# First batch's states: two loads at the head of the scalar and sync queues in place of two loads on GpSimd's queue (block-recurrent cross attention, then a softplus-erf feed-forward block)

## The chip, the cores and the metric

The kernel runs on one core of one Trainium2 chip. The metric is the device time of one execution in microseconds (us); less is better. Engines are named as in the profile: PE is TensorE's matmul and PEld its weight load, DVE is VectorE, ACT is ScalarE, POOL is GpSimd, SP is SyncE. A q behind a name (SPq, ACTq) marks an instruction of that engine's sequencer, such as the issue of a DMA. All data are f32.

## The reference, cut to what matters

```python
B, H, S, Ns, D = (8, 8, 512, 32, 64)          # x: (B,H,S,D)   state: (B,H,Ns,D)
scores = scale * np.matmul(x, state.transpose(0, 1, 3, 2))
a = softmax(scores)                            # exp(s - max) / (sum + 1e-9)
xread = np.matmul(a, state)
scores2 = scale * np.matmul(state, x.transpose(0, 1, 3, 2))
a2 = softmax(scores2)
sread = np.matmul(a2, x)
y = np.concatenate([xread, sread], axis=2)     # 544 rows a batch
x = y.transpose(0, 2, 1, 3).reshape(B * 544, H * D)
h = x @ w_in                                   # 4352 x 512 @ 512 x 2048
g = h * erf(softplus(h))
return g @ w_out                               # 2048 x 512
```

Tokens and states read each other (per batch and head), and the 4352 resulting rows go through a feed-forward block with the activation h · erf(softplus(h)).

## The kernel before, in words

**The work as a whole.** One core takes the batches b = 0 to 7 in order, and at the end the 256 state rows of all batches together. The product of attention weights, states and `w_in` is regrouped: `mixed_part` and `mixed_pair` (lines 447 to 474) first multiply the states with `w_in` into tiles `m`, and the hidden rows are then the attention weights `aT` times `m`. Batch 0 uses plain products (`first0` line 761, `project` line 597), later batches a seven-product scheme (`hidden7`, `project7`). While batch 0 is computed, the weights arrive in 1024-KB blocks as raw words (`weight`, line 127) and are converted by two ACT and three DVE instructions each (lines 144 to 150); the block after next is fetched when one is converted (`on_dve`, line 749).

**What sets the order.** Nothing is left to a planner in this part. From line 89 to line 976 the instructions of PE, DVE, ACT and SP stay in the order in which the code names them (`in_order`, line 78, called in line 976). Each engine takes its own list from the front and stops at an instruction whose inputs are not there. POOL has only a few instructions: it makes the 128×128 identity `ident` (`make_identity`, line 64) and, in this version, issues two DMAs.

**The first loads (lines 106 to 113 and 782 to 784).** The states of batch 0 are 64 KB: for e = 0, 1 (heads of even and odd number) a DMA of 32 KB brings 128 rows of 64 elements into one half of the columns of `st[:, 0, :]`. Both are issued by `nc.gpsimd`, line 109. The tokens of batch 0 are four chunks of 128 tokens, c = 0 to 3, of 256 KB each: ACT issues c = 0, then c = 2; SP issues c = 1, then c = 3 (line 112). Behind them SP issues three weight blocks (line 138 through `fetch`). In this text x0 to x3 are these four loads.

**The first attention (`attention0`, lines 292 to 385), by halves t = 0, 1 of the tokens.** This is PE's list from its first instruction on:

| step | line | what | needs |
|---|---|---|---|
| `warm(8)` | 785, 169 | 16 matmuls of `ident` with itself, results unused | `ident` |
| `turn(0)` | 349, 315 | 8 transposes: chunk 1, then chunk 0 | x1, x0 |
| `states` | 350, 182 | 1 transpose of the states; ACT copies it back into `st` (line 183) | both state loads |
| `warm(1)` | 351 | 2 matmuls of `ident` | |
| `score(0)` | 352, 328 | 16 matmuls, first scores | copied states; `xT` half 0 (ACT line 320, DVE line 321) |
| `turn(1)` | 353, 315 | 8 transposes: chunk 2, then chunk 3 | x2, x3 |
| `warm(3)` | 357 | 6 matmuls of `ident` | |
| `score(1)` | 358, 328 | 16 matmuls, second scores | `xT` half 1 (ACT 320, DVE 321) |
| `warm(28)` | 788 | 56 matmuls of `ident`, results unused | |
| `mixed_part` | 802, 471 | 16 matmuls, states by the first `w_in` block | the converted block |

DVE's list beside it: copy of half 0 (321); two transposes of score(0) (334); copy of half 1 (321); maximum and subtraction of half 0 (342, 343); two transposes of score(1) (334); maximum and subtraction of half 1; sums (347) between the conversion steps of the first weight block (147 to 149); normalisation (232 to 235); two transposes into `aT` (371). ACT copies (320, 183, 338), takes exponentials (344) and does its part of the conversions (144, 146).

**Completion of DMAs.** In the built program the DMAs of the ACT and SP queues take eight completion semaphores in turn, in the order of the code; the two of POOL's queue have semaphores of their own. A DMA that takes a semaphore for the second time may have to wait for the first use to end.

Of the kernel before, what the change touches and what calls it, by code (L numbers as in the profile page):

```python
# [16 lines left out]
def kernel(  # L17
# [17 lines left out]
    nc = tc.nc  # L35
    B, H, S, D = x.shape
# [69 lines left out]
    st = const.tile([P, B, P], F32, name="st")  # L106
    x_t[0] = xin.tile([P, NC, H, D], F32, name="x")
    for e in range(2):
        nc.gpsimd.dma_start(out=st[:, 0, D * e:D * e + D],
                            in_=state[0].rearrange("(i e) n d -> e i n d", e=2)[e])  # L110
    for c in range(NC):
        (nc.scalar, nc.sync)[c % 2].dma_start(
            out=x_t[0][:, c], in_=x[0, :, P * c:P * c + P].rearrange("h p d -> p h d"))
# [951 lines left out]
```

## Time and profile before

| what | us |
|---|---|
| median of 3 runs (lowest, highest) | 734.94 (734.78, 735.68) |
| the profiled execution's own time | 734.94 |
| its span in the profile | 733.2 |
| outside the span (difference) | 1.74 |
| PE busy | 721.7 (98%) |
| PEld busy | 588.0 (80%) |
| DVE busy | 524.7 (72%) |
| ACT busy | 396.1 (54%) |
| POOL busy | 2.1 |

Busy time counts the matmuls of `ident`, too, so a busy PE is not always a PE with useful work. The profile's sections are: busy time by engine; the span in 40 equal slices (18.3 us each), a digit for the busy tenths; the DMA queues (q1 is SP's, q10 is ACT's, q0 is POOL's); the chain that ended last; the costliest groups; the DMA issues with the time from issue to landing. "PEclk" is the share of its full clock that TensorE was granted. The trace behind the page also answers for a stretch of time: the instructions in order, each with the idle time of its engine before it and what ended that idle time; the waits, longest first; the DMAs of one line with the least, median and greatest time to landing; the busy times and the granted clock between two points in time. All points in time here count from the start of the span.

### The profile page before, as it was taken

To read this page: it belongs to the slowest core of one execution; us is meant where nothing else is said; L and a number is where in the kernel's file an instruction comes from. 1 tells how busy PE (TensorE), PEld (TensorE's weight loads), DVE (VectorE), ACT (ScalarE), POOL (GpSimd) and SP (SyncE) were. 2 spreads that over 40 slices of the span, in tenths; PEclk is the share of its full clock that TensorE was granted. 3 is DMA by queue.
4 is the path that set the end of the run, shared out by engine and by line. 5 is a ranking of instruction groups with operands and counts; after the bars stand their busy time and mean duration, and the time that the engine had idled before them with its cause. 6 is when DMAs were issued, how large, how long until landed. Compare 5 with 4: busy or idle time off the path is not lost.

```text
span 733.2 us, 12162 instructions
## 1 busy us (share of the span) xinstructions
PE 721.7 (98%) x5032; PEld 588.0 (80%) x5032; DVE 524.7 (72%) x768; ACT 396.1 (54%) x500; POOL 2.1 (0%) x8
## 2 busy tenths in 40 slices
PE   7999999999999999999999999999999999999997
PEld 6534435888889888988989888988898899999996
DVE  3988887997788666867687669866686756675423
ACT  3899884655646445754355445554565434443340
POOL 1000000000000000000000000000000000000000
PEclk9999999999999999999999999999999999999999
DMA  7577752330043202410061104220121000000001
GB/s 234 169 209 239 216 112 58 87 58 31 14 94 74 51 1 47 98 30 30 1 144 23 37 1 87 64 46 10 30 58 30 30 1 30 1 30 1 30 1 29
DMA packets 138998, 46.40 MB, mean 63 GB/s; under 512 B 126512, under 2 KB 130352, under 8 KB 138944
## 3 DMA queue, kind: packets, MB, share of 16 engines
q1 hardware_dynamic: 136576, 44.85, 24.5%
q10 hardware_dynamic: 2272, 0.72, 0.5%
q8 instruction: 39, 0.64, 0.4%
q14 instruction: 15, 0.12, 0.1%
q0 software_dynamic: 96, 0.07, 0.0%
HBM read 33.03 MB, written 8.91 MB: 57 GB/s over the span
## 4 chain that ended last, share of the span: by engine, by line
PE 88%; DVE 4%; ACT 1%; SPq 1%; issue 1%; DMA 0%; DVEq 0%; ACTq 0%
PE o L650 47%; PE h L543 27%; PE o L600 7%; PE at L457 2%; SPq L432 1%; PE h L457 1%; PE h L764 1%; PE at L197 1%; PE at L471 1%; PE h L277 1%; DVE s L777 0%; PE at L277 0%; DVE hs L771 0%; ACT L774 0%; DVE w_out L148 0%
## 5 line engine op out<-in xcount | busy, mean ns | idle before, releaser
L650 PE MATMUL o<-w_out,s 128*128 128x256 f32 x480 | 118.0, 380 | 0.0
L650 PE MATMUL o<-raw,hs 128*128 128x256 f32 x480 | 117.3, 382 | 0.0
L550 ACT ACTIVATE s<-hs 128x512 f32<-128x512 f32 x120 | 75.4, 630 | 74.3 <-DVE hs L551 74.0
L650 PE MATMUL o<-w_out,hs 128*128 128x256 f32 x480 | 114.1, 380 | 0.0
L650 PEld LDWEIGHTS o<-raw,hs 128*128 128x128 f32 x480 | 89.9, 190 | 22.6 <-issue 10.9
L551 DVE TENSOR_TENSOR hs<-hs,h 128x512 f32<-128x512 f32 x90 | 61.8, 688 | 62.5 <-PE h L543 62.4
L650 PEld LDWEIGHTS o<-w_out,hs 128*128 128x128 f32 x480 | 90.8, 190 | 16.3 <-issue 4.2
L650 PEld LDWEIGHTS o<-w_out,s 128*128 128x128 f32 x480 | 84.6, 191 | 7.9
L551 DVE TENSOR_TENSOR hs<-s,h 128x512 f32<-128x512 f32 x60 | 41.1, 685 | 67.6 <-PE h L543 67.2
L543 PEld LDWEIGHTS h<-aT,m 128*128 128x128 f32 x672 | 83.8, 192 | 4.3 <-issue 1.4
L543 PE MATMUL h<-aT,m 128*128 128x128 f32 x672 | 84.4, 275 | 0.0
L595 DVE TENSOR_TENSOR s<-s,hs 128x2048 f32<-128x2048 f32 (+1 forms) x31 | 68.8, 2219 | 20.4 <-ACT s L593 20.4
L554 ACT COPY s<-h 128x512 f32<-128x512 f32 x29 | 17.0, 586 | 107.6 <-PE h L543 107.6
L600 PE MATMUL o<-w_out,s 128*128 128x512 f32 x128 | 59.1, 600 | 0.6 <-DVE s L777 0.5
L543 PE MATMUL h<-sy,sx 128*128 128x128 f32 x448 | 59.4, 275 | 0.0
L543 PEld LDWEIGHTS h<-sy,sx 128*128 128x128 f32 x448 | 56.7, 192 | 2.0 <-issue 0.5
L593 ACT ACTIVATE s<-s 128x2048 f32<-128x2048 f32 x30 | 57.4, 1912 | 0.3
L559 ACT COPY hs<-h 128x512 f32<-128x512 f32 x29 | 17.0, 586 | 74.8 <-PE h L543 74.8
L650 PE MATMUL o<-raw,s 128*128 128x256 f32 x240 | 56.8, 379 | 0.0
L600 PEld LDWEIGHTS o<-w_out,s 128*128 128x128 f32 x128 | 23.1, 190 | 31.1 <-issue 25.8
L650 PEld LDWEIGHTS o<-raw,s 128*128 128x128 f32 x240 | 43.5, 190 | 4.7
L550 ACT ACT_TABLE_LOAD x31 | 39.8, 1283 | 0.6
(140 smaller groups left out, 917.9 us busy)
## 6 DMA issues: line engine op xcount, KB each, us to landing
raw<-in_moe_w_in_dram SPq DMA_DIRECT2D x8, 1024.0 KB, 5.4
raw<-in_moe_w_out_dram SPq DMA_DIRECT2D x8, 1024.0 KB, 5.0
xq<-in_x_dram SPq DMA_DIRECT2D x112, 64.0 KB, 2.5
x<-in_x_dram SPq DMA_DIRECT2D x56, 128.0 KB, 3.0
out_dram<-ot SPq DMA_DIRECT2D x18, 256.0 KB, 2.1
sc<-xT SPq DMA_DIRECT2D x112, 32.0 KB, 1.9
out_dram<-ot SPq DMA_DIRECT2D x28, 128.0 KB, 1.7
x<-in_x_dram ACTq DMA_DIRECT2D x2, 256.0 KB, 6.0
```

The source lines that it names most:

```text
L197: on_pe = nc.tensor.matmul(out=s2[e][q, :], lhsT=st[r, b, q], rhs=xT[r, i, :], start=True, stop=True)
L277: nc.tensor.matmul(out=sr[q, e, :], lhsT=a2T[:, e, c, q], rhs=xt[:, c, 2 * i + e, :], start=(c == 0), stop=(c == NC - 1))
L457: nc.tensor.matmul(out=ps[k][e][q, :], lhsT=st[r, b, q], rhs=w_in[r, 2 * g:2 * g + 2, i, :], start=True, stop=True)
L543: last = nc.tensor.matmul(out=bank[:, q], lhsT=lhsT, rhs=rhs, start=(first and i == 0 and k == 0), stop=(i == GF - 1 and k == len(ops) - 1 ...
L550: nc.scalar.activation(out=s[:, k], in_=hs[:, k], func=ACTF.Softplus)
L551: add = lambda o, x, y: nc.vector.tensor_tensor(o, x, y, op=ALU.add)
L554: copy(m1, p)
L559: copy(c11, p)
L593: nc.scalar.activation(out=s, in_=s, func=ACTF.Erf)
L595: nc.vector.tensor_tensor(s[:, k], s[:, k], hs[:, k], op=ALU.mult)
L600: nc.tensor.matmul(out=acc[r], lhsT=gT[:, i, P * r:P * r + P], rhs=w_out[:, GF * g + i, :], start=(g == 0 and i == 0), stop=(g == NG - 1 a ...
L650: nc.tensor.matmul(out=acc[bank][:, E2 * c:E2 * c + E2], lhsT=lhs[:, i, :], rhs=rhs[:, g, i, :], start=(first and i == 0 and c == 0), stop ...
```

## The change

In the loop over e, the two state loads are issued by ACT (e = 0) and by SP (e = 1) and no longer by GpSimd. The loop stands ahead of the loads of x, so each of the two is the first DMA of its queue. Nothing else is changed.

```diff
     st = const.tile([P, B, P], F32, name="st")
     x_t[0] = xin.tile([P, NC, H, D], F32, name="x")
     for e in range(2):
-        nc.gpsimd.dma_start(out=st[:, 0, D * e:D * e + D],
-                            in_=state[0].rearrange("(i e) n d -> e i n d", e=2)[e])
+        (nc.scalar, nc.sync)[e].dma_start(out=st[:, 0, D * e:D * e + D],
+                                      in_=state[0].rearrange("(i e) n d -> e i n d", e=2)[e])
     for c in range(NC):
         (nc.scalar, nc.sync)[c % 2].dma_start(
             out=x_t[0][:, c], in_=x[0, :, P * c:P * c + P].rearrange("h p d -> p h d"))
```

In the built program the lists of PE and DVE have the same instructions in the same order. ACT's and SP's lists each have one DMA more, at the front; POOL's list has two DMAs fewer, one of which stood between the two steps that make `ident`. The eight completion semaphores are handed out two places later, so the third weight block of SP (`w_out`, the ninth DMA) now takes the semaphore of ACT's state load and the next one that of SP's; from there on each DMA waits for the same predecessors as before.

## The prediction

> **What bounds the kernel now.** I read the page's 40 slices first, then the waits of the first 20 us, then the first 15 us in order of time, engine by engine. The slices (DVE and POOL beside PE):
>
> ```profile
> PE   7999999999999999999999999999999999999997
> DVE  3988887997788666867687669866686756675423
> POOL 1000000000000000000000000000000000000000
> PEclk9999999999999999999999999999999999999999
> ```
>
> PE is full from the second slice on, in an order written by hand, so this change can gain only by starting the full stretch sooner. The first slice (18.3 us) is the one with a hole. What ends the waits of PE there, by the waits up to 14 us:
>
> ```profile
> PE h L182 <- DMA st<-in_state_dram: 2.7, 1, 2.7
> PE o L169 <- POOL ident masks.py:199: 2.5, 1, 2.5
> ```
>
> Both go back to POOL, and both instructions are touched. PE, ACT and DVE in order of time (start, length, instruction, idle time before it):
>
> ```profile
> 2.54 3.78 PE L169 MATMUL o<-ident 128*128 128x128 f32 x16 [2.54 <-POOL ident masks.py:199]
> ...
> 6.11 1.11 PE L315 MATMUL o<-ident,x 128*128 128x128 f32 x8
> 7.04 0.59 ACT L320 COPY xq<-o 128x512 f32<-128x512 f32 x1 [3.73 <-PE o L315]
> ...
> 9.91 0.45 PE L182 MATMUL h<-ident,st 128*128 128x128 f32 x1 [2.69 <-DMA st<-in_state_dram]
> ...
> 10.72 1.11 PE L328 MATMUL at<-xq,st 64*32 64x256 f32 x16
> ...
> 11.75 0.69 PE L315 MATMUL o<-ident,x 128*128 128x128 f32 x2
> ...
> 13.51 0.69 DVE L321 COPY xq<-h 128x512 f32<-128x512 f32 x1 [0.81 <-PE h L315]
> 14.07 0.82 PE L328 MATMUL at<-xq,st 64*32 64x256 f32 x16
> ```
>
> The reader is to see: turn(0) is over at 7.22, the states' transpose waits until 9.91, and score(0) (10.72) and turn(1) (11.75) stand behind it in PE's list, so DVE gets its copy of half 1 at 13.51. From that copy DVE is the bound: it is busy 3.93 of the 4 us from 16 to 20, 4.90 of 5 from 20 to 25, 4.84 of 5 from 25 to 30, all of 30 to 35, and at 33.36 PE still waits for it (0.24) as the long full stretch begins. The start of DVE L321 at 13.51 is therefore the number that I move; its shift is the shift of the end, unless something with a fixed time comes in between.
>
> The loads, from issue to landing (state loads; then x0 and x2 on ACT; then x1 and x3 on SP):
>
> ```profile
> DMA to landing us min/median/max: 6.7/7.0/7.4
> ...
> DMA to landing us min/median/max: 4.5/6.0/7.4
> ...
> DMA to landing us min/median/max: 3.8/4.8/5.7
> ```
>
> With the issues in order of time (x at 0.74 and 1.25 on both queues, states at 1.29 and 2.42) the landings are x1 4.6, x0 5.2, x3 6.9, x2 8.7, states 8.0 and 9.8. The second half of the states, one of the two smallest loads, lands last.
>
> **The change part by part.**
>
> *Removed.* Two issues on POOL, 0.81 and 0.69 us. The first stood between the two steps of `ident`, the second of which ran at 2.18 to 2.48. Without the 0.81 us `ident` is there at about 1.67 and warm(8) moves from 2.54 to about 1.7 and ends about 0.8 sooner, at 5.1 to 5.3. This decides nothing by itself, since the next step needs x0; cost and gain zero, covered by that wait.
>
> *Added on the queues.* One issue at the head of ACT and of SP. The issue of an x chunk takes 0.45 to 0.49 us when first, so x moves back by one issue place, 0.51 us (0.74 to 1.25), or, if only the queue's own pace counts, by an eighth of a chunk (32 of 256 KB). Chunks land 2.3 us apart on SP (4.6, 6.9) and 3.5 apart on ACT (5.2, 8.7): 0.29 and 0.43 us. So x lands 0.3 to 0.5 later. Against it, POOL's queue no longer competes: in the DMA view of the first 12 us it had 2.9% of 16 engines, 0.35 us. Bounds for x2: 8.7 + 0.3 - 0.35 = 8.65 to 8.7 + 0.5 = 9.2; I take 9.0, nearer the upper end, since the issue place is certain and the relief is not. In the same way x0 lands at 5.2 + 0.4 = 5.6, and the states long before it: they are first in their queues, and by the DMA view of the first 6 us the first bytes flow at 1.9, twice as many from 2.9 on, when the second queue comes in. ACT's table load (2.02) and SP's weight issues (1.86 on) come 0.5 later; the table is first used at 7.04, the first block at 16.09 against a landing at 11.0.
>
> *New waits.* The third weight block's issue (SP, now about 4.1) waits for ACT's state load, landed by then. Behind it on SP there is only the fourth block, which waits for a conversion at 21.9 anyway. Price zero; if the wait did hold, the block (landed 15.9, used 21.88) has 6 us of cover. The later renumbering leaves each DMA its old predecessors: zero.
>
> *The path after the change.* turn(0) ends with x0's four transposes, 5.6 + 0.1 + about 0.8 (the eight took 1.11 by the row) = 6.5; the states' transpose follows at once. ACT copies half 0 (0.59) and then the states (0.27): 7.4. score(0) 7.4 to 8.25 at 0.82, or to 8.5 at 1.11. turn(1) then waits for x2: 9.0. So a wait for x2 takes the place of the wait for the states, and x2 sets the gain: turn(1) begins at 9.0 in place of 11.75. From there to DVE's copy it took 1.76 us before (11.75 to 13.51), at half clock most of the time; turn(0) took 1.15 (6.11 to 7.26) at full clock. I take 1.4, about midway, since the clock of that stretch is open (below): DVE L321 at 10.4. Gain 13.51 - 10.4 = 3.1 us. By the bounds: 9.2 + 1.76 = 10.96 gives 2.5; 8.65 + 1.15 = 9.8 gives 3.7.
>
> *What has a fixed time behind it.* The three weight blocks land at 11.0, 13.4 and 15.9 (issues at 1.86, 2.73, 3.55; 9.1, 10.7, 12.3 to landing) and are first used at 16.09, 19.79 and 21.88; moved up by 3.1, the least slack is 13.0 against 11.0 to 11.5. warm(28) starts with score(1)'s end, so it moves along; it ended at 21.34, the next useful matmul came at 22.04, and ACT took its result only when free at 23.07, 0.35 after it was ready. That is 1.05 us of cover, needed below.
>
> The granted clock is the open term:
>
> ```profile
> 6.30:9.60 3.30, 0.92 (x9) 0.68 (x7) 0.69 (x1) 0.59 (x1) 0.00 (x0) 1.00 1.10 289
> 9.70:13.00 3.30, 3.08 (x25) 2.08 (x26) 0.78 (x2) 0.87 (x3) 0.00 (x0) 0.50 1.05 411
> 13.10:16.50 3.40, 3.40 (x40) 2.84 (x40) 2.92 (x6) 1.54 (x4) 0.00 (x0) 1.00 0.65 263
> ```
>
> (Columns: stretch, its length, busy PE, PEld, DVE, ACT, POOL, then the clock.) After a stretch with PE busy 0.92 of 3.30 the clock was 0.50, after one with 3.08 of 3.30 it was 1.00. After the change the stretch up to 9.7 holds about 2.4 us of PE work (turn(0)'s end, states, score(0), part of turn(1)), between the two. If the next stretch is at half clock, turn(1) takes the 1.76 and about 1.2 us of warm(28) runs at half speed, 0.6 later, within the 1.05 of cover. So it costs 0 to 0.4, which is in the bounds.
>
> **Where the Trainium skill says otherwise.** "DMA: Bandwidth & Descriptors", section "Latency and other measured facts", gives a first byte after about 0.6 us for a DMA of the sync or scalar queue and about 1 us for one of GpSimd's; the same page's "Issuing engines are not separate DMA queues" says that another issuer saves only issue time. By that the states would come some 0.4 us sooner and the time would be about 734.5, an estimate from that page. The rows of the states (6.7 and 7.4 us to landing for 32 KB, against 3.8 for a 256-KB chunk issued earlier) are far from it, and the measurement decides.
>
> "TensorE: Matmul & The Clock Gate", Part 1, says that the clock is set by free-running windows of 3413 ns. By that the half-clock stretch may lie up to 1.7 us later than I placed it; as an estimate the loss would be up to 1.7 - 1.05 = 0.65 us and the time 732.5. One profile can't show that its place varies.
>
> **The rivals.**
> 1. *x2 ceases to be the limit.* Without POOL's packets it lands by 8.2; then PE's own list limits: turn(1) at 8.25, DVE at 9.4, gain 4.1: 730.8. For it: the states' 0.35 us. Against: x2 was already last of its queue by 3.5 us. Chance 0.11.
> 2. *A partial gain.* The half clock falls on turn(1) and the warm matmuls, and x comes 0.5 later still: gain 1.5 to 2.4, some 733.0. Chance 0.09.
> 3. *The small load takes a full chunk's place* (a cost per DMA, not per byte): x2 at 8.7 + 2.3 = 11.0, gain 0.75: 734.2, no change. Against: it has an eighth of a chunk's bytes, in rows of the same length. Chance 0.08.
> 4. *Slower: the state load blocks its queue until it has landed.* For a load of this kind the nearest long row is the later load of the other states (line 118, 56 KB, median 5.1 us to landing behind a weight block). A block of 5.1 us on ACT puts x2 at 13.8, turn(1) 2.05 later than now: 737.0. It decides from 11.75 - 8.7 = 3.05 us of blocking. Against: x3 landed 2.3 us behind x1, x1 taking 3.8 itself, so loads overlap in a queue. Chance 0.04.
>
> **How the numbers follow.** The profiled execution took 734.94 us (span 733.2 and 1.74 around it), which is also the median. Likeliest: 734.94 - 3.1 = 731.8, its own range 731.2 to 732.5, chance 0.68. Rivals 1 and 2 lie beside it on the same side; to hold 8 in 10 I reach from 730.9 to 733.2, which takes in both bounds of the unknown costs. About 0.2% (1.47 us) is what a measurement of this kernel can tell from no change. Faster by more than that: 0.68 + 0.11 + 0.09 = 0.88; within it 0.08; slower 0.04.
>
> **What would show it.** In the profile after, line 182 no longer waits for a DMA and starts near 6.5; the wait of PE in the first slice is one of about 0.7 us in front of line 315 for x; score(0) near 7.4; DVE L321 (half 1) near 10.4; L149 and the first L471 about 3 us sooner; every later row shifted alike. I am wrong if x2 lands past 9.5, if DVE's rows of 13.5 to 33 don't move as a block, or if a weight block becomes a wait at line 144.

## The result and the profile after

The changed kernel takes 732.54 us (median of 6 runs, 731.29 to 733.02) where the kernel before takes 734.99 (6 runs, 734.33 to 735.68): a ratio of 0.9964, 95% interval 0.9951 to 0.9977, or 2.45 us less. It is faster, inside the forecast range (730.9 to 733.2), a hair above the likeliest part of it (731.2 to 732.5), and short of the forecast gain of 3.1 us. The profiled execution took 731.29 us, the fastest of the six, with a span of 729.5; what follows has to explain both that profile and why the median is 1.25 us above it.

The slices of the page after (PE and DVE):

```profile
PE   8999999999999999999999999999999999999998
DVE  5988887997798577867586669866686656674423
```

In PE's row only the first and the last slice are fuller, each by a tenth. PE's longest waits in the first 20 us of the kernel after:

```profile
PE o L169 <- POOL ident masks.py:199: 1.4, 1, 1.4
PE o L315 <- DMA x<-in_x_dram: 1.2, 2, 1.0
```

The wait for the states (2.7) is gone, the one for the identity is 1.2 shorter (2.54 before, 1.35 now), and a wait for x has come. The same steps as before, in order of time:

```profile
1.35 3.70 PE L169 MATMUL o<-ident 128*128 128x128 f32 x16 [1.35 <-POOL ident masks.py:199]
...
6.02 0.66 PE L315 MATMUL o<-ident,x 128*128 128x128 f32 x4 [0.97 <-DMA x<-in_x_dram]
...
6.87 0.66 PE L315 MATMUL o<-ident,x 128*128 128x128 f32 x4 [0.19 <-DMA x<-in_x_dram]
...
7.36 0.27 PE L182 MATMUL h<-ident,st 128*128 128x128 f32 x1
...
8.15 0.80 PE L328 MATMUL at<-xq,st 64*32 64x256 f32 x16 [0.29 <-ACT st L183]
...
8.88 0.44 PE L315 MATMUL o<-ident,x 128*128 128x128 f32 x2
...
10.01 0.69 DVE L321 COPY xq<-h 128x512 f32<-128x512 f32 x1 [0.23 <-PE h L315]
```

The states' transpose follows turn(0) at once (7.36, before 9.91), turn(1) begins at 8.88 (before 11.75) and DVE's copy of half 1 at 10.01 (before 13.51), 3.50 sooner. Every DVE instruction from there to 34.4 us is 3.50 or 3.51 sooner, and nearly all after it 3.46 to 3.49, to the last one: one block, moved. (The span is 3.69 shorter; the other 0.2 comes behind DVE's last instruction.) The loads of x from issue to landing (ACT's two, then SP's two):

```profile
DMA to landing us min/median/max: 4.9/5.7/6.4
...
DMA to landing us min/median/max: 4.4/5.3/6.2
```

With issues at 1.93 and 2.38 on ACT and 1.55 and 2.24 on SP, x1 landed at 6.0 (before 4.6), x0 at 6.8 (5.2), x3 at 8.4 (6.9) and x2 at 8.8 (8.7).

### The profile page after: what moved, and what is told of

Same layout as the page of the kernel before. It is cut to its first block, busy times and chain, and to the rows that moved or that the text cites. A ratio compares the mean times of both kernels' runs of the same rounds, so it can differ in the third digit from the quotient of the medians.

```text
span 729.5 us, 12161 instructions
## 1 busy us (share of the span) xinstructions
PE 720.6 (99%) x5032; PEld 587.0 (80%) x5032; DVE 524.6 (72%) x768; ACT 395.9 (54%) x500; POOL 0.7 (0%) x6
## 4 chain that ended last, share of the span: by engine, by line
PE 91%; DVE 3%; ACT 2%; issue 1%; DVEq 0%; ACTq 0%
PE o L650 49%; PE h L543 28%; PE o L600 7%; PE at L457 2%; PE h L457 1%; PE h L764 1%; PE at L197 1%; PE at L471 1%; PE h L277 1%; DVE s L777 0%; PE at L277 0%; DVE hs L771 0%; ACT L774 0%; DVE w_out L148 0%; DVE xT L389 0%
```

## The experiments

Theory 1: the end moves with the start of DVE L321 (half 1), which is set by x or by PE's list in front of it, whichever is later. Two more parts came out of the runs: 1a, the granted clock of the first 15 us; 1b, weights on SP's queue that overtake x on ACT's. Rivals were the identity, POOL's traffic, and "the states must be first of all". A kernel is compared with the kernel before as measured beside it, since that one gave a median of 734.35 beside one group (a to d), 734.89 (e, f, g, j), 734.64 (h, m) and 734.81 (n). Runs 6, 8 and 9 take the two loads off GpSimd's queue as well; the code shown there leaves that out.

**1. The changed kernel again (a_again).** No edit.

> The changed kernel once more, as the measure for the runs beside it. Theory 1 (the end moves with the start of DVE L321 of half 1, and that start is set by the landing of x2 or by PE's list behind x0, whichever is later): 732.5 us, and in its profile the span is 733.2 less the shift of that copy against 13.51, within 0.3. Rival: the runs of this kernel differ by 1.7 us for a reason later in the kernel; then the copy stands at the same time as in the first profile (10.01) while the span differs.

732.53 us (731.53 to 733.66), beside 734.35 for the kernel before: 0.9981 (0.9970 to 0.9992). Its profile is of another execution, 732.62 us, span 730.8:

```profile
6.45 1.97 PE L315 MATMUL o<-ident,x 128*128 128x128 f32 x8 [1.31 <-DMA x<-in_x_dram]
...
8.99 1.29 PE L328 MATMUL at<-xq,st 64*32 64x256 f32 x16
...
11.35 0.69 DVE L321 COPY xq<-h 128x512 f32<-128x512 f32 x1 [0.24 <-PE h L315]
```

The same 16 score matmuls took 1.29 us here and 0.80 in the first profile. The first record of full clock stands at 10.26 us here, and at 4.85 there. Copy and span are both 1.3 later (11.35 and 730.8), so theory 1 holds and the two executions differ at the start, not later. turn(1) begins at 10.21 here, 1.2 after x2 (9.0), so x2 sets nothing in it. x0 landed at 6.8 in both; the half clock up to 10.26 makes the difference.

**2. The identity late (b_ident_late).** One instruction ahead of `make_identity` (the tile `st` is made there, too); the columns are overwritten by `load_st` later:

```diff
+    nc.gpsimd.memset(st[:, 1:B, :], 0.0)
     make_identity(nc, ident)
```

> A memset of 128x896 on POOL ahead of the identity brings it back to about 2.4 us, where the kernel before had it; the state loads stay on ACT and SP. Theory 1: the first transpose waits for x1 (6.02) and x0 (6.87), so warm(8) ending at 6.1 in place of 5.05 costs 0 to 0.2 us: 732.5 to 732.7. Rival 'the identity' (the gain comes from POOL being free for the identity): 0.9 to 1.1 us of the gain goes: 733.5.

731.54 us (731.18 to 732.05). Neither: it is 1.0 faster than the changed kernel beside it. warm(8) now ran from 2.13 to 5.91 and met x1 (5.88) with no idle time of PE:

```profile
2.13 3.78 PE L169 MATMUL o<-ident 128*128 128x128 f32 x16 [2.13 <-POOL ident masks.py:199]
...
5.92 1.79 PE L315 MATMUL o<-ident,x 128*128 128x128 f32 x8
```

In the changed kernel it ended at 5.05 and PE stood idle for 1.0 (first profile) or 1.3 us (second).

**3. More matmuls in place of that idle time (f_warm10).**

```diff
-    warm(8)
+    warm(10)
```

> The changed kernel with warm(10) in place of warm(8): 20 matmuls of the identity, not 16, so that PE is busy until x1 lands (about 6.0) though the identity is early. Theory 1a (the early identity left PE idle from 5.05 to 6.0, and in some places of the clock's windows that keeps the half clock one window longer): 731.5, as with the late identity (731.54), and a spread below 1 us. Rival (the late identity helped for a reason of POOL's or of the loads' own): 732.5 as the changed kernel, spread 1.5 to 2 us.

731.52 us (731.31 to 732.09) beside 734.89: 0.9960 (0.9948 to 0.9973). The identity is as early as in the changed kernel, POOL is free, and the time is that of the late identity. So it is PE's idle time between the warm matmuls and x1 that costs 1.0 us in the median; in the profiled run 0.65 us of it is left, as x1 landed only at 6.2. The idle time itself decides nothing in the first profile (x0 ends the step). That the clock does, in the executions where its windows lie badly (theory 1a), is read from the profile of run 1, the only one of such an execution of the changed kernel.

**4. The same idle time in the kernel before (e_before_again, h_before_filled).** The second edit:

```diff
         copies(0, turn(0))
+        warm(8)
         states(range(1), ps_h, "h")
```

> The kernel before once more, for a second profile and its spread. Its 34 runs beside the last four kernels lie in two heaps, about 732.6 to 733.7 and 734.0 to 735.7. Theory 1a (the place of the windows of the granted clock differs from run to run, and in one part of the places the states' wait drops PE to half clock for the next window, which costs the scores): two heaps again, 13 of 34 or so in the lower; the profile of a run below 733.7 has no half-clock stretch between the states and the warm matmuls, and one above 734 has. Rival: the heaps come from the landing of the states; then line 182 starts 1.5 to 2 us apart in the two profiles, and the clock is alike.

734.88 us (732.67 to 735.57); only 1 of 12 runs lay in the lower heap. Its profile (734.87 us) has half clock from 11.58 to 14.99, right behind the states' wait, and line 182 at 10.03.

> The kernel before with warm(8), 16 more matmuls of the identity, between turn(0) and the states' transpose, where PE waits for the states from about 7.2 or 8.0 to 9.9. The loads and their landings are as before. Theory 1a (that wait costs twice: 2.0 to 2.7 us of waiting, and a window at half clock behind it in most places of the windows): line 182 still at 9.9 to 10.4, no half-clock stretch behind it, DVE L321 of half 1 at 11.8 to 12.4, time 732.8 to 733.6 with most runs within 1 us of each other. Rival (the waiting alone is the loss): 734.7 as the kernel before, or more, since the added matmuls can only delay.

733.65 us (732.69 to 733.87) beside 734.64: 0.9984 (0.9975 to 0.9993). Line 182 stands where it stood, but nothing behind it is at half clock:

```profile
9.99 0.30 PE L181 MATMUL h<-ident,st 128*128 128x128 f32 x1 [1.25 <-DMA st<-in_state_dram]
...
12.37 0.69 DVE L320 COPY xq<-h 128x512 f32<-128x512 f32 x1 [0.20 <-PE h L314]
```

(Its lines are one lower.) The copy moves from 13.06 or 13.51 to 12.37 with the states as late as ever. The median is 0.05 us above the expected range. So about 1.0 us of the kernel before went to the half clock that followed the wait; that the wait alone was the rest is argued, not tested by itself.

The lower heap of the kernel before has 24 of the 94 runs beside these experiments (13 of 34, 3 of 20, 1 of 15, 6 of 13, and 1 of the 12 above), and no profile fell into it. But the granted clock of each run is on record: these 24 (732.54 to 733.81 us) have 0.999 or 1.000 of the full clock, the 70 others (733.98 to 735.72) 0.994 to 0.998, and one window of 3.41 us at half clock is 0.002 of the span. So the upper heap has such a window, as both profiles of it show, and the lower has none. Most of the lower heap is near 732.6, though, 1.0 below the filled kernel, which has no such window either; what that is, an earlier landing of the states for one, is not shown. For the reader it means that the change gains against three executions in four, while the best of the kernel before were already as short as the changed kernel's median.

**5. POOL's traffic brought back (d_pool_traffic).** The old two loads are issued as well, into columns that are overwritten later; nobody waits for them:

```diff
+    for e in range(2):
+        nc.gpsimd.dma_start(out=st[:, 1, D * e:D * e + D],
+                            in_=state[0].rearrange("(i e) n d -> e i n d", e=2)[e])
```

> The changed kernel with the old two loads on POOL's queue kept as well; they bring the same 64 KB into columns that are overwritten later, and nobody waits for them. It brings back POOL's packets and the late identity, without the wait. Theory 1: x2 lands 0.2 to 0.5 us later: 732.6 to 733.0. Rival 'traffic' (POOL's queue slowed x, and that was the loss): the most of the gain goes: 734.3 or above.

732.92 us (732.19 to 734.57). It has the late identity, so it stands beside run 2 (731.54): the two loads cost 1.4 us. In its profile x1 landed at 6.9, x0 at 8.3, x2 at 10.2, against 5.9, 6.9 and 8.8 in run 2, and the copy stood at 11.50 against 10.20. The time is the expected one by luck: x2 came 1.4 later and not 0.2 to 0.5, and the late identity gave 1.0 back. Against the kernel before the ratio is 0.9990 (0.9979 to 1.0001), so that part of the gain is kept is read from the profile (copy at 11.50 against 13.06 and 13.51), not from the times. Nor is this the traffic of the kernel before, as the states are brought twice here and POOL's first load comes sooner: issued at 1.29 in both, its first packet came at 2.74 and it landed at 5.4, in the kernel before at 6.05 and 8.0. There x0 and x1 were issued ahead of it (0.74), here behind it (1.54 and 1.93). So the late landing is no fixed cost of POOL's queue; why the packets came so late there stays open, and so does traffic's share of the gain.

**6. The states behind the first chunks (c_behind_first_chunks).**

```diff
     for c in range(NC):
         (nc.scalar, nc.sync)[c % 2].dma_start(out=x_t[0][:, c], ...)
+        if c < 2:
+            (nc.scalar, nc.sync)[c].dma_start(out=st[:, 0, D * c:D * c + D], ...)
```

> Each state load goes behind the first x chunk of its queue (ACT: x0, states, x2; SP: x1, states, x3). Theory 1: x1 and x0 land about 1 us sooner (4.6 to 5.3), the states at about 6, before turn(0) is over at 6.2 to 6.6, so the states' transpose waits less than 0.3 us; x2 lands at 8.8 to 9.0 as before, so DVE L321 of half 1 stands at 9.9 to 10.1 and the time is 732.3, the same within 0.3. Rival 'the states must be first of all' : the states' transpose waits 1 us or more and the time is 733.5 or above.

734.50 us (733.30 to 735.57) beside 734.35: 1.0012 (1.0002 to 1.0022), a miss, and not for the rival's reason. The states' transpose stood at 6.63, after a wait of 0.6, and score(0) at 7.29, sooner than in the changed kernel. But x2 landed at 11.5. PE's longest wait, and the busy times during it and behind it (stretch, length, PE, PEld, DVE, ACT, POOL, clock):

```profile
PE o L315 <- DMA x<-in_x_dram: 3.6, 1, 3.6
```

```profile
8.00:11.40 3.40, 0.00 (x0) 0.00 (x0) 0.78 (x2) 0.70 (x2) 0.00 (x0) 1.00 1.05 401
11.50:14.80 3.30, 3.25 (x22) 3.03 (x30) 1.25 (x2) 0.58 (x1) 0.00 (x0) 0.50 0.94 380
```

3.6 us without a matmul, then half clock. The first weight packets (2048 bytes) came on SP's queue at 5.9, those of x (256 bytes) went on there to 7.1 and on ACT's to 11.1, with x2 the last. That made theory 1b: which queue ends first counts, and not whether the states lead.

**7. Both state loads at the head of ACT's queue (j_both_on_act), and then the weights behind x (n_weights_behind).**

```diff
-        (nc.scalar, nc.sync)[e].dma_start(out=st[:, 0, D * e:D * e + D],
+        nc.scalar.dma_start(out=st[:, 0, D * e:D * e + D],
```

> The changed kernel with both state loads at the head of ACT's queue, none on SP's. Theory 1b: ACT is later by one more load and SP earlier by one, so the weights start about 6.4 while x2 is only half brought: x2 lands at 10 to 12 and the time is 734 to 735.5, the gain of the change is gone though the states are still the first loads of their queue. Rival 'states first is what counts': 732.5, and at most 0.5 us above.

740.01 us (739.04 to 741.00) beside 734.89: 1.0074 (1.0059 to 1.0089), 5.1 us slower than the kernel before, with the states first of all, and 4.5 above the expected range. The first weight packets came on SP's queue at 4.0, and not only x2 (16.2) but even x0 was held, to 14.7:

```profile
14.73 1.12 PE L315 MATMUL o<-ident,x 128*128 128x128 f32 x4 [8.74 <-DMA x<-in_x_dram]
```

The second kernel issues the first three weight blocks on ACT, behind x2:

```diff
+        queue = nc.scalar if len(fetched) < 3 else nc.sync
-        fetched.append(nc.sync.dma_start(out=raw.rearrange(...
+        fetched.append(queue.dma_start(out=raw.rearrange(...
```

> As the kernel with both state loads at the head of ACT's queue (740.0), but the first three weight blocks are issued by ACT behind x2, so that no weights run beside x0 and x2. Theory 1b (weights on the other queue, started while x is still under way, hold x back): x0 lands at 6.5 to 7.5 in place of 14.7, x2 at 8.5 to 9.5; ACT's own three more issues push its table load to about 7.5, so DVE L321 of half 1 stands at 10.3 to 11.3 and the time is 731.6 to 733.0; a first weight block landing past 13 may add up to 1. Rival (the loads of the states, or ACT's queue, are slow by themselves): x0 still lands at 10 or later and the time is 736 or above.

733.58 us (732.24 to 734.14) beside 734.81: 0.9990 (0.9975 to 1.0005).

```profile
7.42 1.11 PE L315 MATMUL o<-ident,x 128*128 128x128 f32 x4 [1.44 <-DMA x<-in_x_dram]
```

x0 landed at 7.4 in place of 14.7 and x2 at 8.1, with the same state loads ahead of them: 1b holds, and a slow queue is ruled out. The time is 0.6 above the expected range: in the profiled run full clock came only at 13.86, and turn(1) to the copy took 2.0 us (10.33 to 12.33) in place of the 1.13 at full clock.

**8. Both state loads on SP behind x1 (g_both_on_sp).**

```diff
     for c in range(NC):
         (nc.scalar, nc.sync)[c % 2].dma_start(out=x_t[0][:, c], ...)
+        for e in range(2) if c == 1 else ():
+            nc.sync.dma_start(out=st[:, 0, D * e:D * e + D], ...)
```

> ACT: x0, x2; SP: x1, both state loads, x3, weights. In the run with the states behind the first chunk of both queues SP began the weights at 6.0 while x2 was still under way on ACT, and x2 landed at 11.5. Theory 1b (weights of 2048-byte packets that start on SP before ACT has brought x2 hold x2 back; what counts is which queue ends first): here ACT ends first, x2 lands at 7.0 to 8.0, x3 at 7.5 to 8.2, DVE L321 of half 1 at 9.0 to 9.5, time 730.6 to 731.2. Rival 'the states must be first of all': the states land at 5.5 to 6.5, behind x1, and the time is 733 or above.

731.91 us (731.64 to 733.13) beside 734.89: 0.9968 (0.9957 to 0.9979). That is 0.7 above the expected range. x2 landed at 7.3, as expected, but x3 at 8.7 and the states only at 7.9: PE waited 1.4 us for them, and the profiled run (732.76) had half clock from 9.32 to 12.73 behind that wait. The order of the queues was right, the price of two state loads in a row on one queue was not.

**9. Short queues of equal length (m_x2_shared).** ACT: x0, states, half of x2; SP: x1, states, the other half of x2, x3, weights.

```diff
+    for e, queue in enumerate((nc.scalar, nc.sync)):
+        first_x(queue, e)
+        queue.dma_start(out=st[:, 0, D * e:D * e + D], ...)
+    first_x(nc.scalar, 2, slice(0, H // 2))
+    first_x(nc.sync, 2, slice(H // 2, H))
+    first_x(nc.sync, 3)
```

> ACT: x0, states e = 0, heads 0 to 3 of x2; SP: x1, states e = 1, heads 4 to 7 of x2, x3, weights. As with the states behind the first chunk of both queues, x1 and x0 land at 4.7 and 5.3, but ACT's queue is shorter by half a chunk and ends before SP begins the weights. Theories 1 and 1b: x2 and x3 land at 7.8 to 8.3 in place of 11.5 for x2, score(0) at 7.3 to 8.0, DVE L321 of half 1 at 9.1 to 9.6, time by the rule of the ten profiles (span = that start + 719.5, and 1.8 around it) 730.4 to 730.9, faster than every version so far. The first weight block lands at about 11.4 and is wanted at 11.8; if it lands later than that, the time is up to 0.5 longer. Rival 'states first of all': 733 or above, as a load of x stands ahead of both.

730.64 us (730.60 to 730.95) beside 734.64: 0.9947 (0.9934 to 0.9959), the fastest version, inside its expectation:

```profile
6.68 0.30 PE L182 MATMUL h<-ident,st 128*128 128x128 f32 x1 [0.49 <-DMA st<-in_state_dram]
...
7.93 0.44 PE L315 MATMUL o<-ident,x 128*128 128x128 f32 x2
...
9.06 0.69 DVE L321 COPY xq<-h 128x512 f32<-128x512 f32 x1 [0.20 <-PE h L315]
```

The states, behind a chunk of x, cost a wait of 0.5, and x2 (7.5) is there before PE reaches turn(1). The five runs lie within 0.35 us.

## Why the prediction held, point by point

The main step, that the wait for the states goes and the whole block behind DVE's copy moves up, was right. The way to the copy was not, and that the time still fell in the range is in part luck: errors of opposite sign, in a range that had been widened for a partial gain. In run 1, which is near the median, the copy stood at 11.35, past the bound of 10.96.

**The number that was moved.** In thirteen profiles the span less the start of DVE L321 (half 1) is nearly one number, over a start from 9.06 to 19.65:

| kernel | start of the copy | span | difference |
|---|---|---|---|
| before, again | 13.51, 13.06 | 733.17, 733.10 | 719.66, 720.03 |
| after, again | 10.01, 11.35 | 729.48, 730.84 | 719.47, 719.49 |
| late identity; warm(10) | 10.20; 10.03 | 729.68; 729.52 | 719.49; 719.49 |
| POOL's traffic | 11.50 | 731.14 | 719.64 |
| behind first chunks | 13.55 | 733.13 | 719.59 |
| both on SP; both on ACT | 11.02; 19.65 | 730.97; 739.15 | 719.96; 719.50 |
| weights behind | 12.33 | 731.98 | 719.65 |
| before, filled; x2 shared | 12.37; 9.06 | 732.03; 728.83 | 719.66; 719.77 |

This step was right: nothing with a fixed time came in between, and the weights, the last steps and the new completion semaphores cost nothing that shows. The two largest differences (720.03 and 719.96) are of the profiles in which half clock went on longest behind the copy, 1.9 and 1.7 us.

**"x lands 0.3 to 0.5 later."** Mis-sized. x1, x0 and x3 landed 1.4 to 1.6 later. The issue of a state load took 0.75 us on SP and 1.15 on ACT, where I had put in the 0.45 to 0.49 of an x chunk, and x's issues moved from 0.74 to 1.55 and 1.93, not to 1.25. That makes 0.8 of the delay on SP and 1.2 on ACT; where the other 0.6 and 0.4 come from is not shown. turn(0) therefore ended 1.0 later than forecast, and score(0) began at 8.15, not 7.4.

**"x2 at 9.0."** It landed at 8.8, though it too was issued 1.1 later. POOL's packets were gone, and the first weight packets came later, too (7.4, before 6.4); no run parts the two. But in that profile PE reached turn(1) only as x2 landed (8.88), so x2 did not set the gain alone; the late x0 did as much. In run 1 x2 was there 1.2 us before it was wanted, so in the usual execution "x2 sets the gain" is wrong.

**"turn(1) to the copy, 1.4."** 1.13 at full clock (8.88 to 10.01). turn(1) began 0.1 sooner than forecast and took 0.3 less, so the copy came at 10.01 and not 10.4, in the profiled run. That score(0) came 0.75 late did not show, as the forecast had 0.5 to 0.75 of slack in front of x2: luck.

**"Cost and gain zero" for the earlier identity.** Wrong, and the reason why the median is 0.7 above the forecast. (The sum was off as well: by its own terms warm(8) would have ended at 5.5, not at 5.1 to 5.3; the identity came 1.2 sooner, not 0.8, and it ended at 5.05.) The 1.2 us that POOL gave back opened an idle stretch of PE at 5.05, and where the windows of the clock lie badly, full clock comes one window late (in run 1 at 10.26 in place of 6.84), which moves the copy to 11.35. Run 3 closes the stretch and gains 1.0. I had weighed the half clock only behind the states' wait, and priced it at 0 to 0.4. Rival 2, a partial gain by half clock, has the gain of the run of 732.62 (2.3) but not the place: the half clock lay on turn(0) and score(0), and was over as turn(1) began.

**Rival 4, the state load that blocks its queue.** A loss of its kind is real: with both loads on ACT the time is 740. Its mechanism is not: with the weights taken off the other queue, x0 lands at 7.4 behind the same two loads, so it is not they that block it.

**Queues and clock windows.** The rule of the Trainium skill that another issuer saves only issue time ("DMA: Bandwidth & Descriptors", "Issuing engines are not separate DMA queues") would have given 734.5, an estimate; the measurement (732.54) decides against it as a price here. What bears on run 7 is that x0 landed at 14.7 beside the weights of the other queue and at 7.4 without them. The Trainium skill, "DMA: Bandwidth & Descriptors", section "Queues, rings and completion order", says that each DMA engine takes turns between the queues, one packet at a time. If the 2048-byte and 256-byte packets of the trace are packets in that sense, the large ones of one queue take most of an engine's time from the small ones of the other, which agrees.

Full clock is first recorded at 4.85, 5.08, 7.27 and 10.26 us in four profiles whose PE work begins within 0.8 us, and the half-clock stretches inside the first 20 us last 3.41 us or three times that. The Trainium skill, "TensorE: Matmul & The Clock Gate", Part 1, calls the windows free-running, and that agrees. The estimate of 732.5 that I gave by that page came out near the median by luck, with the half clock in another place.

## What to carry to other kernels

Find the first instruction from which everything moves as one block, and price a change at the start of a kernel by that instruction alone. When a small load is moved ahead of others, count the issue time of that load's own shape, and look at which queue then ends first: here a queue that went on to 2048-byte packets early starved the 256-byte ones on the other (x0 at 14.7 in place of 7.4). An idle stretch of PE ahead of the first full clock is worth filling even where the next step does not need it: here it was 1.0 us in the median and most of the spread.

## What the runs showed of the hardware that was not expected

- The issue of the first state load of a queue takes 0.72 to 0.76 us on SP and 1.13 to 1.16 on ACT, whether first in the queue (after) or second (runs 6, 8 and 9); the second on the same queue takes 0.55 or 0.56. An x chunk of eight times the bytes takes 0.45 to 0.51 when first.
- A state load leaves 4 completion packets in the trace on ACT's and SP's queues, an x chunk 16. The outermost dimension of the state load's source is 4. The Trainium skill, "DMA: Bandwidth & Descriptors", section "Why a DMA increments its semaphore by 16 and not by 1", says that a DMA is spread over the largest number of engines, up to 16, that divides the outermost dimensions of both its sides; the 4 packets agree. Few engines for the states would fit their late landing in run 8, which no run tried by itself.
- Laid on the clock records of the thirteen profiles, the first 20 us fall into windows of 3.41 us, and the busy time of PE in one (summed from its rows) goes with the clock of the next, by two different bounds. (Windows ahead of the first record count as half clock.) At half clock, windows with PE busy 3.14 us or more were followed by full clock, and those with 2.95 (weights behind), 2.37, 2.21 and 2.10 (after, again) were not. At full clock, 1.96 (after) and more kept it, 1.41 and less lost it, and 1.83 kept it in one profile where 1.85 lost it in another. So in these profiles it took a nearly unbroken window to win full clock, and about half a window of idle time to lose it.
